# Fewer warm-up products, and a half slot's last tile in columns of 512 and 256 with its rows scattered in thirds

## The chip, the cores and the metric

One core of a Trainium2 chip runs the whole program. The metric is device time in microseconds (us). TensorE multiplies, ScalarE and VectorE empty its accumulators (PSUM) and prepare operands, GpSimd computes lists and issues the indirect DMAs (gathers and scatters of rows by an index), SyncE issues the plain loads.

## The reference, cut to what matters

Eight batches of 448 positions with 12 heads of 64 go through a sigmoid attention; its result, 3584 rows of 768, goes through a mixture of eight experts, of which each row takes one:

```python
scores = np.matmul(q, k.transpose(0, 1, 3, 2)) / 8 - np.log(448)
x = np.matmul(1 / (1 + np.exp(-scores)), v)   # then 3584 rows of 768
e_idx = np.argmax(x @ w_gate, axis=1)
for e in range(8):
    mask = e_idx == e
    h = np.maximum(x[mask] @ w1[e], 0.0)      # 768 -> 1024
    ye = h @ w2[e]                            # 1024 -> 768
    out[mask] = gate_w[mask, None] * eom[mask, e, None] * ye
```

## The kernel before

**Attention.** It comes first. `attention` runs over units of one 128-position chunk of keys for one pair of heads: `scores(u)` multiplies into one of two accumulators, ScalarE applies the sigmoid to it (L603), and two units later `values` multiplies by v. Ahead of the loop SyncE issues the first loads of q, k and v, and TensorE runs 20 products of a zeroed tile (L671 and L672), whose result nobody reads; the first `scores` stands behind them in TensorE's order and needs the first k and q.

**Slots.** The rows of one expert are taken in slots: big ones of 448 rows, then, for what is left of each expert, half slots of 256 rows (TM), under an `If` each. With these inputs two half slots run; the prediction calls them H0 and H1. `slot` writes out each engine's order by hand. In layer 1 (L537 on) eight column blocks of h are made; with the first four, GpSimd gathers the rows of the next slot, eight gathers of 32 x 4 row quarters for a half slot (`gather_rows`, L381), and w2 is split into a high and a low part. Behind layer 1 VectorE transposes the gathered rows (`turn_x`, L425), which needs all gathers landed, and they are split (`split_x`: a cast on ScalarE, L406, a subtraction on VectorE, L407). H1 does this too, for a slot that doesn't follow.

**Layer 2 of a half slot.** Two tiles of 128 rows, t = 0 and 1, each in two column halves, n = 0 and 1: four groups of 24 products of 384 columns, into one of three PSUM banks in turn. Behind a group ScalarE scales it by the row's weight into `y` (L490); in the last group of a half slot ScalarE scales 192 columns (L487) and VectorE the other 192 (L488). Between these scalings stand on ScalarE and VectorE the last `split_x` (behind the first group) and `split_w1` for the next slot (behind the first three). When both halves of a tile are in `y`, `scatter` (L495) issues one indirect DMA of its 128 rows of 3072 bytes into `out`. Scatters and gathers stand on GpSimd's one queue in the order of the code: the scatters of H0 ahead of the gathers of H1.

**Order between DMAs.** The framework puts in a semaphore wait where two instructions touch the same memory. `out` is written by every scatter; the indirect DMAs take eight completion semaphores (DMASW0 to DMASW7) in turn.

Of the kernel before, what the change touches and what calls it, by code (L numbers as in the profile page):

```python
# [11 lines left out]
I32 = mybir.dt.int32  # L12
AF = mybir.ActivationFunctionType
ALU = mybir.AluOpType
# [10 lines left out]
NT = B * S  # L25
# [6 lines left out]
TM = 256  # L32
# [19 lines left out]
def r32(ap):  # L52
    return ap.bitcast(F32)


class Kernel:
# [68 lines left out]
    def constants(self):  # L125
        nc = self.nc
        cp = self.const = self.pool("const")
        dram = self.pool("dram", space=DRAM)
        self.x_dram = dram.tile([NT, DM], F32, name="x_dram")
        self.lst = dram.tile([E * CAP, W], I32, name="lst")  # L130

        self.bias_s = cp.tile([128, 1], F32, name="bias_s")
        nc.vector.memset(self.bias_s, -math.log(S))
        nc.scalar.activation(self.warm_t(cp), self.bias_s, AF.Sigmoid)
        iota = lambda t, pattern, base=0, cm=0: nc.gpsimd.iota(
            t, pattern=pattern, base=base, channel_multiplier=cm, allow_small_or_imprecise_dtypes=True)
        self.rev = cp.tile([64, NB, E], F32, name="rev")
        iota(self.rev, [[0, NB], [-1, E]], E)
        self.last = cp.tile([64, 32], F32, name="last")
        nc.gpsimd.memset(self.last, 0.0)  # L140
        for i in range(2):
            iota(self.last[32 * i:32 * i + 32, 0:1], [[0, 1]], -1, CAP)
        self.step = cp.tile([64, 2], F32, name="step")
        self.turned = cp.tile([32, 32], F32, name="turned")
        self.run = cp.tile([1, E], F32, name="run")
        self.one = cp.tile([64, 1], F32, name="one")
        nc.gpsimd.memset(self.one, 1.0)
        self.ebase = cp.tile([1, E], F32, name="ebase")
        iota(self.ebase, [[CAP, E]])
        self.ids = cp.tile([1, E], F32, name="ids")  # L150
        iota(self.ids, [[1, E]])
        self.kts = cp.tile([1, KT], F32, name="kts")
        iota(self.kts, [[TB, KT]], TM)
        self.meta = cp.tile([128, B, NCH, W], I32, name="meta")
        for i in range(4):
            r, at = slice(32 * i, 32 * i + 32), HS * (i % 2) + 32 * NCH * (i // 2)
            for w, q, o in ((0, 4, 0), (1, 4, 1), (2, 4, 2), (3, 4, 3), (4, 1, 0)):
                nc.gpsimd.iota(self.meta[r, :, :, w], pattern=[[q * S, B], [q * 32, NCH]], base=q * at + o,
                               channel_multiplier=q)
        self.zero = cp.tile([128, 128], BF16, name="zero")  # L160
        nc.gpsimd.memset(self.zero, 0.0)
        self.eps = cp.tile([64, NB], F32, name="eps")
        nc.gpsimd.memset(self.eps, 1e-9)
        self.one8 = cp.tile([1, E], F32, name="one8")
        nc.gpsimd.memset(self.one8, 1.0)
        self.taken = cp.tile([1, E], F32, name="taken")
        nc.gpsimd.memset(self.taken, 0.0)
        self.tab_e, self.scattered = [], []
        slots = EARLY + LATE_N
        self.lts = cp.tile([128, slots, 4, 2], I32, name="lts")  # L170
        self.ltb = cp.tile([128, E, 2, 2], I32, name="ltb")
        self.lxs = cp.tile([128, slots, GB_], I32, name="lxs")
        self.lxb = cp.tile([128, E, GM], I32, name="lxb")
        self.slots = cp.tile([1, 2, LATE_N], F32, name="slots")
        for i, st in enumerate((1, TB)):
            iota(self.slots[:, i], [[st, LATE_N]])
        self.route_tiles()
# [296 lines left out]
    def layer2(self, s, t, n, y, last=False):  # L474
        nc = self.nc
        tk = slice(128 * t, 128 * t + 128)
        c = slice(384 * n, 384 * n + 384)
        hh, hl = self.hs
        ps = self.take("y", self.psy)[:, 0:384]
        for f in range(8):  # L480
            wh, wl = self.w2_at(f, c)
            nc.tensor.matmul(ps, hh[:, f, tk], wh, start=(f == 0), stop=False)  # L482
            nc.tensor.matmul(ps, hh[:, f, tk], wl, start=False, stop=False)  # L483
            nc.tensor.matmul(ps, hl[:, f, tk], wh, start=False, stop=(f == 7))  # L484
        w = r32(s["lt"][:, t, 1:2])
        if last and n == 1:
            nc.scalar.activation(y[:, 384:576], ps[:, 0:192], AF.Copy, scale=w)  # L487
            nc.vector.tensor_scalar(y[:, 576:768], ps[:, 192:384], w, None, ALU.mult)  # L488
        else:
            nc.scalar.activation(y[:, c], ps, AF.Copy, scale=w)  # L490
        if n == 1:
            self.scatter(s["lt"][:, t, 0:1], y)

    def scatter(self, at, y):
        self.nc.gpsimd.indirect_dma_start(  # L495
            out=self.out, out_offset=bass.IndirectOffsetOnAxis(ap=at, axis=0),
            in_=y, in_offset=None, bounds_check=NT - 1, oob_is_err=False)

    def layer2_rest(self, s):
        nc = self.nc  # L500
# [14 lines left out]
    def slot(self, cur, nxt, side=None, begun=False, hint=None):  # L515
        nx = None
        if nxt is not None:
            nx, rows, sure = nxt() if callable(nxt) else nxt
            last = -(-nx["lx"].shape[1] // 2) - 1
        n = 32 * cur["lx"].shape[1]  # L520
        for f in range(8):
            if n == TB and f == begun:
                self.change_step()
            self.layer1(f, n, begun and f == 0)
            if nx is not None and f <= last:
                self.gather_rows(nx, 2 * f, rows, 1)
                self.gather_rows(nx, 2 * f + 1, rows, 0)
                if f == last and not sure:
                    self.nc.gpsimd.drain()
            if side is not None:  # L530
                next(side, None)
            if 1 <= f < 5:
                self.split_w2(f - 1)
                if f > 1:
                    self.load_w1(nx, f - 2)
        for k in range(3):
            self.turn_x(nx, k)  # L537
        self.split_x(nx, 0)
        self.split_x(nx, 1)
        for i in range(2 * (n // 128)):  # L540
            t = i // 2
            if hint is not None and i == 5:
                more = self.nc.values_load(self.more[0:1, hint[1]:hint[1] + 1], engines=[ET.PE], min_val=0, max_val=1)
                self.tc.mark_branch_hint_location(hint[0], hint=more, engines=[ET.PE])
            self.layer2(cur, t, i % 2, self.ys[(t + (t > 0 and n % 128 > 0)) % 2], n == TM and t == 1)
            if i == 0:
                self.split_x(nx, 2)
            if i < 3 and nx is not None:
                self.split_w1(i)
                for k in range(i, 4 if i == 2 else i + 1):  # L550
                    self.load_w2(nx, k)
            if side is not None:
                next(side, None)
            if i == 1 and n % 128:
                self.layer2_rest(cur)
        return nx

    def attention(self, pool):
        nc = self.nc
# [4 lines left out]
        t = lambda n, shape: pool.tile(shape, F32, name=n)  # L564
# [3 lines left out]
        at = [t(f"a{i}", [128, 2, S]) for i in range(3)]  # L568
# [19 lines left out]
        def load_v(g):  # L588
            b, hp = divmod(G * g, NPAIR)
            v = vv[g % 3]  # L590
            nc.sync.dma_start(v[:, :, 0:3], self.vm[b, hp:hp + G].rearrange("g p c j d -> p g c j d"))
            for i in range(G):
                nc.sync.dma_start(v[half[i], i, 3], self.ve[b, hp + i])
# [74 lines left out]
        for g in (1, 2):  # L668
            load_qk(g)
            load_v(g)  # L670
        for _ in range(20):  # L671
            nc.tensor.matmul(self.ps_o[1][0][:, 0:256], warm[:, 0:128], warm, start=True, stop=True)  # L672
        LAG = 2
        for u in range(U * NG + LAG):
            g, i = divmod(u, U)
# [169 lines left out]
```

## Time and profile before

| | us |
|---|---|
| median of 3 runs | 773.86 |
| lowest, highest | 773.79, 775.93 |
| the profiled execution | 774.47 |
| its span, first to last instruction | 772.7 |
| TensorE busy | 759.8 |
| ScalarE, VectorE, GpSimd busy | 374.2, 398.9, 263.4 |

Times in rows are from the start of the span. A busy TensorE is not TensorE at its peak. A timeline row has start, duration, engine, line, operation, output and inputs, and in brackets how long the engine had been idle and what ended that. "POOLq" and "PEldq" are the queues that feed GpSimd and TensorE's weight loads: an event there is a wait for semaphores, which may stand beside work that was issued ahead of it. "DMA to landing" is the time from the start of the issuing instruction to the last semaphore increment.

### The profile page before, as it was taken

The numbers are of one execution on the slowest core, as the hardware profiler recorded it, in microseconds if no ns is written. First come the engines' busy times: TensorE is split into PE (matmuls) and PEld (weight loads), VectorE is DVE, ScalarE is ACT, GpSimd is POOL, SyncE is SP. The second block draws the span as 40 slices with busy tenths as digits, with TensorE's granted clock in tenths as the row PEclk, the third lists the DMA queues.
The fourth block names the chain that finished last, engine by engine and source line by source line (L and its number), as shares of the span: only waits on it lengthen the run. The fifth ranks groups of instructions, "written<-read, shape, count | busy, mean of one in ns | idle before, by whom it ended". The sixth has DMA issues, their size and how long they took to land. (4 is left out here: it accounts for less than half of the span.)

```text
span 772.7 us, 14875 instructions
## 1 busy us (share of the span) xinstructions
PE 759.8 (98%) x5826; PEld 585.0 (76%) x5826; DVE 398.9 (52%) x715; ACT 374.2 (48%) x429; POOL 263.4 (34%) x375
## 2 busy tenths in 40 slices
PE   9999999999999999999999999999999999989996
PEld 4444444444434389999999999999999999989996
DVE  1364646556686769523624615615615615614564
ACT  5666666666777733422523523524424524424454
POOL 5002112020443346258346137127127127215161
PEclk9999999999999999999999999999999999999998
DMA  8474756656796546447346346346345354354531
GB/s 283 122 212 130 208 138 176 188 149 171 261 300 200 143 108 200 137 110 222 114 154 215 113 137 215 118 135 210 115 139 176 116 174 155 103 195 151 181 137 41
DMA packets 73464, 126.53 MB, mean 164 GB/s; under 512 B 15375, under 2 KB 53263, under 8 KB 73376
## 3 DMA queue, kind: packets, MB, share of 16 engines
q1 hardware_dynamic: 62768, 100.18, 42.8%
q0 software_dynamic: 9680, 24.53, 9.5%
q8 instruction: 50, 0.82, 0.4%
q10 hardware_dynamic: 928, 0.69, 0.4%
q14 instruction: 38, 0.31, 0.1%
HBM read 108.77 MB, written 23.09 MB: 171 GB/s over the span
## 5 line engine op out<-in xcount | busy, mean ns | idle before, releaser
L603 ACT ACTIVATE a<-ps,bias_s 128x896 f32<-128x896 f32 x168 | 168.8, 1007 | 86.6 <-PE ps L601 86.0
L381 POOL DMA_INDIRECT plain<-x_dram,lxs x112 | 137.1, 1224 | 74.5 <-ACT h L467 24.3
L601 PE MATMUL ps<-q,k 64*64 64x448 f32 x1344 | 157.7, 540 | 0.7 <-ACT a L603 0.7
L610 PE MATMUL ps<-a,v 64*64 64x448 f32 x1344 | 156.2, 536 | 0.0
L455 PE MATMUL ps<-rounded 128*128 128x448 f32 (+1 forms) x432 | 151.3, 350 | 2.8 <-ACTq L798 2.8
L457 PE MATMUL ps<-rounded 128*128 128x448 f32 (+1 forms) x432 | 150.6, 349 | 0.0
L456 PE MATMUL ps<-rounded 128*128 128x448 f32 (+1 forms) x432 | 150.5, 348 | 0.0
L482 PE MATMUL ps<-w2h,h 128*128 128x384 f32 x400 | 133.9, 335 | 0.3 <-DVE y L512 0.2
L484 PE MATMUL ps<-w2h,h 128*128 128x384 f32 x400 | 133.7, 334 | 0.0
L483 PE MATMUL ps<-w2l,h 128*128 128x384 f32 x400 | 133.6, 334 | 0.0
L468 DVE SCALAR_TENSOR_TENSOR h<-ps,h 128x384 fp32r<-128x384 f32 (+2 forms) x128 | 45.2, 390 | 164.0 <-ACT h L467 164.0
L407 DVE TENSOR_TENSOR rounded<-plain,rounded 128x2048 fp32r<-128x2048 f32 (+5 forms) x63 | 97.6, 1570 | 55.2 <-ACT rounded L406 55.0
L467 ACT ACTIVATE h<-ps 128x448 fp32r<-128x448 f32 (+1 forms) x72 | 36.7, 510 | 162.0 <-PE ps L457 158.9
L601 PEld LDWEIGHTS ps<-q,k 64*64 64x64 f32 x1344 | 50.6, 134 | 76.0 <-issue 70.3
L610 PEld LDWEIGHTS ps<-a,v 64*64 64x64 f32 x1344 | 51.4, 133 | 74.9 <-issue 72.4
L406 ACT CAST rounded<-plain 128x2048 fp32r<-128x2048 f32 (+5 forms) x63 | 83.0, 1333 | 28.3 <-DVE plain L425 26.4
L495 POOL DMA_INDIRECT out<-y,lts x28 | 31.7, 1133 | 186.0 <-ACT y L490 125.3
L455 PEld LDWEIGHTS ps<-rounded 128*128 128x128 f32 x432 | 82.3, 191 | 8.6 <-ACTq L798 3.1
L457 PEld LDWEIGHTS ps<-rounded 128*128 128x128 f32 x432 | 82.2, 190 | 5.0
L456 PEld LDWEIGHTS ps<-rounded 128*128 128x128 f32 x432 | 82.2, 190 | 4.9
L482 PEld LDWEIGHTS ps<-w2h,h 128*128 128x128 f32 x400 | 75.1, 188 | 1.1 <-DVE y L512 0.5
L483 PEld LDWEIGHTS ps<-w2l,h 128*128 128x128 f32 x400 | 75.1, 188 | 0.1
(141 smaller groups left out, 680.9 us busy)
## 6 DMA issues: line engine op xcount, KB each, us to landing
plain<-w SPq DMA_DIRECT2D x40, 768.0 KB, 4.8
plain<-w SPq DMA_DIRECT2D x27, 1024.0 KB, 5.1
k<-kT SPq DMA_DIRECT2D x23, 448.0 KB, 3.5
q<-qT SPq DMA_DIRECT2D x23, 448.0 KB, 6.2
x_dram<-xt SPq DMA_DIRECT2D x30, 336.0 KB, 5.8
v<-vm SPq DMA_DIRECT2D x24, 384.0 KB, 5.3
plain<-w SPq DMA_DIRECT2D x6, 512.0 KB
plain<-x_dram,lxs POOLq DMA_INDIRECT x112, 4.4
```

What stands on the lines that cost most here:

```text
L381: self.paced(self.nc.gpsimd.indirect_dma_start(out=self.xg[:, g], out_offset=None, in_=x4, in_offset=bass.IndirectOffsetOnAxis(ap=s["lx"][ ...
L406: self.nc.scalar.copy(hi, raw)
L407: self.nc.vector.tensor_tensor(lo, raw, r32(hi), ALU.subtract)
L455: nc.tensor.matmul(ps, wh[d][:, c], xh[:, d, 0:n], start=(d == 0), stop=False)
L456: nc.tensor.matmul(ps, wh[d][:, c], xl[:, d, 0:n], start=False, stop=False)
L457: mm = nc.tensor.matmul(ps, wl[d][:, c], xh[:, d, 0:n], start=False, stop=(d == 5))
L482: nc.tensor.matmul(ps, hh[:, f, tk], wh, start=(f == 0), stop=False)
L483: nc.tensor.matmul(ps, hh[:, f, tk], wl, start=False, stop=False)
L484: nc.tensor.matmul(ps, hl[:, f, tk], wh, start=False, stop=(f == 7))
L601: qk = nc.tensor.matmul(ps[half[h], j, 0:S], k[half[j], e, o:o + 64], q[half[j], e], start=True, stop=True)
L603: self.beat[0] = nc.scalar.activation(at[u % 3], ps[:, :, 0:S], AF.Sigmoid, bias=self.bias_s, scale=1.0 / math.sqrt(D)).ins
L610: nc.tensor.matmul(self.ps_o[e][h][half[j], 0:S], v[half[h], e, c, j], a[half[h], j], start=(i in ((0, 3 if h else 4)[e],)), stop=(i == (2 ...
```

## The change

**Start.** The loop of warm-up products runs 11 times instead of 20.

**Half slots' last tile.** `layer2` with `last` (only t = 1 of a half slot) takes columns 0 to 512 and 512 to 768 instead of two halves of 384. ScalarE scales both alone; VectorE's part (L488) goes. The tile's rows are scattered in thirds of 256 columns (1024 bytes a row): two scatters behind the first group, one behind the second. The output is seen as 10752 rows of 256 for that, and the row numbers 3 * row + k are made by three 128x1 operations on VectorE (`third_rows`), behind `split_x(nx, 2)`. Tile 0 and the big slots scatter whole rows as before.

```diff
+        self.thirds = cp.tile([128, 3], I32, name="thirds")
...
     def layer2(self, s, t, n, y, last=False):
...
-        c = slice(384 * n, 384 * n + 384)
+        c = slice(*((0, 512), (512, 768))[n] if last else (384 * n, 384 * n + 384))
...
-        ps = self.take("y", self.psy)[:, 0:384]
+        ps = self.take("y", self.psy)[:, 0:c.stop - c.start]
...
-        w = r32(s["lt"][:, t, 1:2])
-        if last and n == 1:
-            nc.scalar.activation(y[:, 384:576], ps[:, 0:192], AF.Copy, scale=w)
-            nc.vector.tensor_scalar(y[:, 576:768], ps[:, 192:384], w, None, ALU.mult)
-        else:
-            nc.scalar.activation(y[:, c], ps, AF.Copy, scale=w)
-        if n == 1:
+        nc.scalar.activation(y[:, c], ps, AF.Copy, scale=r32(s["lt"][:, t, 1:2]))
+        if last:
+            for k in range(c.start // 256, c.stop // 256):
+                self.scatter(self.thirds[:, k:k + 1], y[:, 256 * k:256 * k + 256], 3)
+        elif n == 1:
             self.scatter(s["lt"][:, t, 0:1], y)
 
-    def scatter(self, at, y):
+    def third_rows(self, at):
+        for k in range(3):
+            self.nc.vector.tensor_scalar(self.thirds[:, k:k + 1], at, 3.0, float(k), ALU.mult, ALU.add)
+
+    def scatter(self, at, y, parts=1):
         self.nc.gpsimd.indirect_dma_start(
-            out=self.out, out_offset=bass.IndirectOffsetOnAxis(ap=at, axis=0),
-            in_=y, in_offset=None, bounds_check=NT - 1, oob_is_err=False)
+            out=self.out.rearrange("n (i e) -> (n i) e", i=parts),
+            out_offset=bass.IndirectOffsetOnAxis(ap=at, axis=0),
+            in_=y, in_offset=None, bounds_check=parts * NT - 1, oob_is_err=False)
...
             if i == 0:
                 self.split_x(nx, 2)
+                if n == TM:
+                    self.third_rows(cur["lt"][:, 1, 0:1])
...
-        for _ in range(20):
+        for _ in range(11):
```

GpSimd's queue at the end of H0 and the start of H1's gathers, with the semaphores that each instruction waits for (`y_..` is a tile's scaled rows, `ltb` holds row numbers, `lxb` the next slot's gather indices). Before:

```order
L381 DMA plain<-x_dram,lxb 128x192 [waits DMASW3_49,Activation_49]
L495 DMA out<-y_2665,ltb 3584x768 [waits DMASW4_49,Activation_49,Pool_49]
L495 DMA out<-y_2666,ltb 3584x768 [waits DMASW5_49,DMASW4_49,DVE_49]
L805 COMPARE_AND_BRANCH
L381 DMA plain<-x_dram,lxb 128x192 [waits DMASW6_49,PE_49]
L381 DMA plain<-x_dram,lxb 128x192 [waits DMASW7_49,Activation_49]
```

GpSimd's queue at the same place after the change:

```order
L382 DMA plain<-x_dram,lxb 128x192 [waits DMASW3_49,Activation_49]
L498 DMA out<-y_2657,ltb 3584x768 [waits DMASW4_49,Activation_49,Pool_49]
L498 DMA out<-y_2658,thirds 10752x256 [waits DMASW4_49,DMASW5_49,DVE_49,Activation_49]
L498 DMA out<-y_2658,thirds 10752x256 [waits DMASW6_49,DMASW5_49,DVE_49]
L498 DMA out<-y_2658,thirds 10752x256 [waits DMASW6_49,DMASW7_49,DVE_49,Activation_49]
L811 COMPARE_AND_BRANCH
L382 DMA plain<-x_dram,lxb 128x192 [waits DMASW0_49,PE_49]
```

Tile 0's scatter completes on DMASW4 and the ones behind it on DMASW5, 6 and 7; each waits for the earlier use of its own semaphore, and for that of the scatter ahead of it. Three scatters stand where one stood, ahead of H1's gathers.

VectorE in layer 2 of H0, behind the transposes of the gathered rows. Before:

```order
L407 TENSOR_TENSOR rounded<-plain,rounded 128x2x256 [waits PE_49,Activation_49] x3
L407 TENSOR_TENSOR rounded<-plain,rounded 128x2048 [waits DMAHW5_49,Activation_49]
L407 TENSOR_TENSOR rounded<-plain,rounded 128x2048 [waits DMAHW6_49,Activation_49]
L407 TENSOR_TENSOR rounded<-plain,rounded 128x2048 [waits DMAHW7_49,PE_49,Activation_49]
L488 TENSOR_SCALAR y_2666<-ps,ltb 128x192 [waits Activation_49,Pool_49]
```

VectorE at the same place after the change:

```order
L408 TENSOR_TENSOR rounded<-plain,rounded 128x2x256 [waits PE_49,Activation_49] x3
L495 TENSOR_SCALAR thirds<-ltb 128x1 [waits Pool_49]
L495 TENSOR_SCALAR thirds<-ltb 128x1 x2
L408 TENSOR_TENSOR rounded<-plain,rounded 128x2048 [waits DMAHW5_49,Activation_49]
L408 TENSOR_TENSOR rounded<-plain,rounded 128x2048 [waits DMAHW6_49,Activation_49]
L408 TENSOR_TENSOR rounded<-plain,rounded 128x2048 [waits DMAHW7_49,PE_49,Activation_49]
```

The three index operations stand ahead of the splits of w1, and the scaling behind them is gone. ScalarE's order is as before, with 512 and 256 columns in the last two scalings.

## Rows read from the trace of the kernel before

**Rows 1.** The page, busy us, share of the span, instructions.
```profile
PE 759.8 (98%) x5826; PEld 585.0 (76%) x5826; DVE 398.9 (52%) x715; ACT 374.2 (48%) x429; POOL 263.4 (34%) x375
```
**Rows 2.** ScalarE's timeline, second scaling of H0, then three of H1.
```profile
723.70 0.58 ACT L490 ACTIVATE y<-ps,ltb 128x384 f32<-128x384 f32 x1
...
757.62 0.58 ACT L490 ACTIVATE y<-ps,ltb 128x384 f32<-128x384 f32 x1 [1.27 <-PE ps L484]
...
765.94 0.42 ACT L487 ACTIVATE y<-ps,ltb 128x192 f32<-128x192 f32 x1 [1.79 <-PE ps L484]
```
**Rows 3.** VectorE's timeline, transposes of H0 and H1, last scaling of H1.
```profile
718.86 1.90 DVE L425 STREAM_TRANSPOSE plain<-plain 128x512 f32<-128x512 f32 x3 [2.64 <-DMA plain<-x_dram,lxb]
...
750.50 1.90 DVE L425 STREAM_TRANSPOSE plain<-plain 128x512 f32<-128x512 f32 x3 [0.37 <-DMA plain<-x_dram,lxb]
...
766.40 0.42 DVE L488 TENSOR_SCALAR y<-ps,ltb 128x192 f32<-128x192 f32 x1
```
**Rows 4.** GpSimd's timeline, scatters of H0 and H1, first and last gather of H1.
```profile
725.11 1.78 POOL L495 DMA_INDIRECT out<-y,ltb  x1 [11.85 <-ACT y L490]
...
734.55 0.98 POOL L381 DMA_INDIRECT plain<-x_dram,lxb  x1 [0.30 <-issue]
...
747.48 0.94 POOL L381 DMA_INDIRECT plain<-x_dram,lxb  x1 [0.31 <-issue]
758.48 1.09 POOL L495 DMA_INDIRECT out<-y,ltb  x1 [10.06 <-ACT y L490]
767.10 0.99 POOL L495 DMA_INDIRECT out<-y,ltb  x1 [7.53 <-DVE y L488]
```
**Rows 5.** Views of L495 at 767, 758, 725, 679; of L381 at 700, 741.
```profile
DMA to landing us min/median/max: 3.7/3.7/3.7
...
L495 POOLq EVENT_SEMAPHORE  x1: 4671/4671/4671, 758.3 to 758.3; - x1
...
DMA to landing us min/median/max: 4.5/4.5/4.5
...
DMA to landing us min/median/max: 6.6/6.6/6.6
...
DMA to landing us min/median/max: 3.0/3.0/3.0
...
DMA to landing us min/median/max: 2.6/2.7/2.7
...
L381 POOL DMA_INDIRECT plain<-x_dram,lxb x4: 942/1851/1860, 741.0 to 747.5; - x4
...
DMA to landing us min/median/max: 3.6/3.8/3.8
```
**Rows 6.** A big slot: view of L495 at 672, timelines of VectorE and GpSimd.
```profile
L495 POOLq EVENT_SEMAPHORE  x1: 6633/6633/6633, 672.1 to 672.1; - x1
...
677.56 0.61 DVE L512 SCALAR_TENSOR_TENSOR y<-ps,lts,y 64x384 f32<-64x384 f32 x1 [0.93 <-ACT y L511]
...
679.51 0.93 POOL L495 DMA_INDIRECT out<-y,lts  x1 [5.71 <-issue]
```
**Rows 7.** Start: views of L672, L601; TensorE's timeline; then 697 to 700.3 (windows, L455).
```profile
L672 PE MATMUL ps<-rounded x20: 415/415/582, 1.2 to 5.5; 128*128 128x256 f32 x20
...
L601 PEldq EVENT_SEMAPHORE  x1: 51/51/51, 4.5 to 4.5; - x1
...
L601 PE MATMUL ps<-q,k x16: 537/774/1006, 5.8 to 7.8; 64*64 64x448 f32 x16
...
6.60 1.35 PE L601 MATMUL ps<-q,k 64*64 64x448 f32 x8
...
8.70 0.61 PE L601 MATMUL ps<-q,k 64*64 64x448 f32 x4 [0.37 <-ACT a L603]
...
697.00:700.30 3.30, 3.30 (x17) 3.30 (x17) 0.00 (x0) 0.30 (x1) 0.00 (x0) 0.50 0.18 70
...
L455 PE MATMUL ps<-rounded x5: 415/415/419, 697.1 to 699.7; 128*128 128x256 f32 x5
```

## The prediction, made before the change was run

> **What bounds the kernel now.** I read the page's busy times first: TensorE is busy for 98% of the span [rows 1], so until the last product the time is TensorE's, and whatever moves its first real product moves the end by as much. Then the timelines of the last stretch, ScalarE's, VectorE's and GpSimd's: the kernel ends on a scatter of result rows, not on a product. Two half slots run; call them H0 and H1. In H1 ScalarE scales the first half of the last columns at 765.94 for 0.42, VectorE's part starts only at 766.40 for 0.42 [rows 2, 3], the scatter starts at 767.10 [rows 4] and lands 3.7 later, at 770.8 [rows 5]; the span ends at 772.7, so 1.9 lie behind the last landing.
>
> Next I read what a scatter waits for, in the view of its line. GpSimd's queue stands from 758.3 for 4.67 us, that is until 762.97, at a wait that belongs to the last scatter; the scatter of the tile before it started at 758.48 and lands 4.5 later, at 762.98 [rows 4, 5]. In a big slot it costs time today: the wait from 672.1 lasts 6.63, to 678.7, VectorE had finished those rows at 678.17, and the scatter starts at 679.51 [rows 6]. So a scatter into `out` waits until the scatter before it has landed, and starts 0.8 later. Before the change that hides behind products. In the program after it, the order in front.md shows each third waiting for the semaphore of the third before: three scatters that follow each other by landing plus 0.8.
>
> **The change part by part.**
>
> *Eviction and products of the last tile.* 24 products of 512 and 24 of 256 columns replace 48 of 384: as many products and as many columns, so TensorE's end stays, and 512 or 256 columns are costed at zero by both counts. ScalarE's two scalings end 8.32 apart over two groups of products [rows 2], 4.16 each, so the wider group ends a third later: its scaling starts near 757.62 + 5.55 = 763.2 and, from 0.42 for 192 and 0.58 for 384 columns [rows 2], takes 0.69; the last takes 0.47 instead of 0.42 + 0.42 on two engines. By itself that gives back 0.4. The three 128x1 index operations lie on VectorE between splits where it waits for ScalarE; zero.
>
> *One landing of a third (131 KB).* Not in the trace. Nearest rows: a 98 KB gather lands in 2.7, a 64-row scatter of 196 KB in 3.0, both on quiet queues [rows 5]; I take 2.8. Beside weight loads a whole tile takes 6.6, and gathers beside VectorE's splits 3.8 [rows 5]: the upper ends. The Trainium skill, DMA: Bandwidth & Descriptors, Anatomy of one DMA, gives a fixed 2.0 us plus bytes over 436 KB per us. By that slope the 196 KB scatter's 3.0 would become 2.85 for a third, and a third would land 0.6 before a whole tile; by it the sum below would be 0.1 higher, and the three thirds still pay the fixed part three times.
>
> *H0: the thirds delay H1's gathers.* The first tile's scatter of H0 starts at 725.11 and lands 6.6 later, at 731.7 [rows 4, 5]; third A starts at 732.5 (its columns are scaled by 730). Weight loads still fill the DMA engines; between 2.8 and 6.6 I take 5.0: A lands at 737.5, B starts at 738.3 and takes 3.8, C starts at 742.9. The eight gathers of H1 stand behind C on GpSimd's queue. C lies beside VectorE's splits and takes 1.85, as the gathers there do [rows 5]; with the 0.3 between two of GpSimd's DMAs [rows 4] the first gather starts at 745.05 and not at 734.55, 10.5 late. Before, the eight take 13.9 because most lie beside those splits; now one does (2.15 with its gap), the others take 1.25, so the eighth starts at 754.7, lands at 757.4, and VectorE's transposes begin at 757.7 instead of 750.50 [rows 3, 4]: 7.2 late.
>
> *H1: ScalarE's queue.* Behind the transposes stand, on ScalarE in order, two casts of x, the first scaling, two casts, the second scaling. In H0 that took 4.84 from transposes to second scaling (718.86 to 723.70) [rows 2, 3] with nothing idle between. So H1's second scaling starts at 757.7 + 4.84 = 762.55, not 757.62. TensorE doesn't feel it: its last group needs the bank of the first scaling, free by 760.7, and starts after 763. But the first tile's scatter starts 1.4 (H0) or 0.9 (H1) after that scaling began [rows 2, 4]; with 1.2 at 763.75. It lands in 3.0 to 4.5 [rows 5]; 3.7 gives 767.45.
>
> *H1: the chain of thirds.* A at 767.45 + 0.8 = 768.25 (its columns are scaled by 765.7); B at 768.25 + 2.8 + 0.8 = 771.85; C at 775.45, landed at 778.25; with the 1.9 behind it the span ends at 780.2. The tail costs 7.5.
>
> Its ends: A in H0 at 2.8 instead of 5.0, B and C there at 3.0, the first tile at 3.0 and 0.9 put the end near 777.2 (+4.5); A in H0 at 6.6, the first tile at 4.5 and H1's thirds at 3.8 each put it at 784.7 (+12.0).
>
> *Eleven warm-up products.* Twenty start between 1.2 and 5.5 at 0.22 each; 256 columns take 415 ns there, and the first score products 1006 falling to 537 ns by 7.8 [rows 7]: the pace of 1.2 GHz, then of 2.4 (at 697 to 700, where the profile has a granted clock of 0.50, 256 columns also take 415 [rows 7]; the page's clock row shows full speed from the start, so here I go by the products). The nine that go took 9 x 0.213 = 1.9. The last semaphore that the first score product needs is passed at 4.5 [rows 7], so it can start at about 4.5 instead of 5.80, and TensorE stands from 3.8 to 4.5. At the low level a unit of scores takes two rounds of 0.75 to 0.8 (5.80 to 6.60 is the first [rows 7]), two units 3.05: 7.56. The third starts at 8.70 now, when ScalarE has finished the first unit [rows 7]; then it could start at 7.56, 1.1 earlier. That is the gain if the clock rises when it does now, near 7.4. If instead it rises as long after the first product without a gap as now (6.2 after 1.23, so at 10.7), then from 7.56 to 10.7 every us does half its work: 1.57 lost, 0.4 slower in all. I take +0.4, since the pause is new and nothing before it had raised the clock by 4.5; bounds -1.1 and +0.6. The Trainium skill, TensorE: Matmul & The Clock Gate, What's actually happening, says that activity releases the clock and that the monitor doesn't start anew with the kernel, so the point differs between executions. By that the term would vary between my two values from run to run; one trace can't show it.
>
> *Sum.* 7.5 + 0.4 = 7.9. The profiled execution took 774.47 for a span of 772.7, so 1.8 lie around the span; it would take 782.4. It is 0.6 above the median, 773.86, which becomes 781.8.
>
> **The rivals.** (1) *Only H1's thirds count.* If H1's gathers start so little late that the transposes begin before 752.8 (2.3 late), ScalarE catches up. Then the first tile's scatter lands at 762.98 as now, A starts at 763.2 + 0.69 + 0.28 = 764.15, B at 767.75, C at 771.35, landed at 774.15, end 776.1: +3.4, and with the start 777.7. Against it: H0's first tile lands only at 731.7, so C can't be out before 739 even at 2.8 each. (2) *The thirds flow as meant*, the other side: A and B lie under the last 2.9 us of products and C starts 0.28 after the last scaling, at 766.7, carries a third and lands in 2.8: end 771.4, -1.3; with +0.4 it gives 773.0, with -1.1 it gives 771.5, faster. It decides only if two links fit between 764.15 and 766.7, under 1.3 each, or if the wait isn't for the landing; the shortest link in the rows is 2.7 + 0.8. (3) *Worse:* thirds slow in H1 too, 786. (4) *The clock rises as early as now:* the forecast less 1.5, 780.3; it changes no sign but in rival 1, where it gives 776.2.
>
> **How the numbers follow.** The forecast, 781.8 (777 to 785): 0.72, of which a third has the early clock. Rival 1: 0.15. Rival 2: 0.06. Rival 3: 0.07. The range 777.0 to 785.0 leaves out rivals 2 and 3 and the lower third of rival 1, 0.18. About 0.3%, 2.3 us, is what a measurement of this kernel can tell from no change: faster below 771.5, slower above 776.2. Rival 2 with the early clock gives faster 0.03; its rest and rival 1 with the early clock give same 0.08; slower 0.89.
>
> **What would show it.** On GpSimd: in each half slot four scatters that start one landing plus 0.8 apart, 3.6 in H1; H1's first gather at about 745; the transposes at about 758; ScalarE's second scaling near 762.5. TensorE's last product near 766 as now, and some 14 us between it and the end instead of 7. At the start the first score product at 4.5 and the third unit at 7.6, and a pace of 1006 ns that lasts past 7.5. The forecast is wrong if a third starts before the one ahead of it has landed, or if the last product moves by more than 2.

## The result and the profile after the change

The changed kernel takes 782.29 us (781.52 to 783.84), the kernel before 774.55 (773.79 to 775.93) beside it: a ratio of 1.0114 [1.0099, 1.0128]. The medians lie 7.7 apart; the ratio would be 8.8 us, and the two profiled spans lie 9.2 apart. The forecast was 781.8 in 777 to 785. The total came out by luck: the change of the half slots was taken some 2 us too cheap or more, the shorter start 1 to 2 us too dear.

The profiled execution of after took 783.84 with a span of 781.9. The page's busy times, to be held against [rows 1]:

```profile
PE 759.3 (97%) x5817; PEld 582.1 (74%) x5817; DVE 398.5 (51%) x719; ACT 374.0 (48%) x429; POOL 272.2 (35%) x379
```

GpSimd's timeline (start us, us, what; in brackets the idle time before and what ended it), to be held against [rows 4]:

```profile
725.00 1.77 POOL L498 DMA_INDIRECT out<-y,ltb  x1 [11.84 <-ACT y L486]
732.47 2.28 POOL L498 DMA_INDIRECT out<-y,thirds  x1 [5.70 <-ACT y L486]
739.48 1.83 POOL L498 DMA_INDIRECT out<-y,thirds  x1 [4.73 <-issue]
743.51 2.13 POOL L498 DMA_INDIRECT out<-y,thirds  x1 [2.20 <-ACT w2h L407]
745.94 1.86 POOL L382 DMA_INDIRECT plain<-x_dram,lxb  x1 [0.30 <-issue]
...
764.01 2.46 POOL L498 DMA_INDIRECT out<-y,ltb  x1 [7.43 <-ACT y L486]
769.76 1.33 POOL L498 DMA_INDIRECT out<-y,thirds  x1 [3.29 <-DMA out<-y,ltb]
774.20 0.97 POOL L498 DMA_INDIRECT out<-y,thirds  x1 [3.10 <-issue]
777.36 0.97 POOL L498 DMA_INDIRECT out<-y,thirds  x1 [2.20 <-DMA out<-y,thirds]
```

In both half slots four scatters now stand 3.2 to 7.5 us apart, and GpSimd is idle between them. The first gather of H1 starts at 745.94 and not at 734.55. GpSimd's busy time rose by 9 us, which costs nothing by itself; the spacing is the cost. In the chain of what ended last stands a third's landing, 2.31 after its start:

```profile
774.20 2.31 DMA out<-y,thirds
```

The views of the other scatters of H1 have 2.5 for the last third, 3.7 for the first and 4.8 for the tile ahead of them (764.01):

```profile
DMA to landing us min/median/max: 2.5/2.5/2.5
...
DMA to landing us min/median/max: 3.7/3.7/3.7
...
DMA to landing us min/median/max: 4.8/4.8/4.8
```

VectorE's timeline, the transposes of H1, which start 7.9 later than in [rows 3]:

```profile
758.44 1.90 DVE L426 STREAM_TRANSPOSE plain<-plain 128x512 f32<-128x512 f32 x3 [7.72 <-DMA plain<-x_dram,lxb]
```

ScalarE's timeline, the second and the last scaling of H1, to be held against [rows 2]:

```profile
763.16 0.57 ACT L486 ACTIVATE y<-ps,ltb 128x384 f32<-128x384 f32 x1
...
767.79 0.48 ACT L486 ACTIVATE y<-ps,ltb 128x256 f32<-128x256 f32 x1
```

TensorE hardly feels it. By its timeline the last product starts at 766.18; then 15.7 us pass to the end at 781.9:

```profile
766.18 0.28 PE L485 MATMUL ps<-w2h,h 128*128 128x256 f32 x1
```

TensorE's timeline at the start of after, the counterpart of [rows 7]:

```profile
1.23 2.71 PE L678 MATMUL ps<-rounded 128*128 128x256 f32 x11 [1.23 <-DVE rounded L671]
4.14 3.87 PE L607 MATMUL ps<-q,k 64*64 64x448 f32 x24 [0.19 <-DMA q<-qT]
8.04 0.98 PE L616 MATMUL ps<-a,v 64*64 64x448 f32 x8
```

The value products (L616) start at 8.04; in the kernel before they start at 9.50, behind the third unit of scores at 8.70 [rows 7]. The start was a gain and not the small loss that I had chosen. TensorE's waits in after (line waited for: total, times, longest) show, beside 0.2 for the first q, two that the kernel before does not have:

```profile
PE ps L513 <- ACT y L486: 1.3, 1, 1.3
...
PE ps L458 <- DVE rounded L408: 0.4, 1, 0.4
```

The first lies at 371 us, in a big slot that the diff does not touch, the second in layer 1 of H1. The experiments take them up.

### The profile page after: what moved, and what is told of

It is laid out like the page before. It is cut to its first block, busy times and chain, and to the rows that moved or that the text cites. A ratio compares the mean times of both kernels' runs of the same rounds, so it can differ in the third digit from the quotient of the medians.

```text
span 781.9 us, 14874 instructions
## 1 busy us (share of the span) xinstructions
PE 759.3 (97%) x5817; PEld 582.1 (74%) x5817; DVE 398.5 (51%) x719; ACT 374.0 (48%) x429; POOL 272.2 (35%) x379
## 5 line engine op out<-in xcount | busy, mean ns | idle before, releaser
L382 POOL DMA_INDIRECT plain<-x_dram,lxs x112 | 140.1, 1251 | 73.5 <-ACT h L468 23.0
L616 PE MATMUL ps<-a,v 64*64 64x448 f32 x1344 | 156.4, 537 | 0.0
L483 PE MATMUL ps<-w2h,h 128*128 128x384 f32 (+2 forms) x400 | 134.1, 335 | 0.3 <-DVE y L516 0.2
L485 PE MATMUL ps<-w2h,h 128*128 128x384 f32 (+2 forms) x400 | 134.0, 335 | 0.0
L484 PE MATMUL ps<-w2l,h 128*128 128x384 f32 (+2 forms) x400 | 133.9, 335 | 0.0
L616 PEld LDWEIGHTS ps<-a,v 64*64 64x64 f32 x1344 | 51.4, 133 | 75.1 <-issue 72.3
```

The costliest lines, as they stand in the source:

```text
L382: self.paced(self.nc.gpsimd.indirect_dma_start(out=self.xg[:, g], out_offset=None, in_=x4, in_offset=bass.IndirectOffsetOnAxis(ap=s["lx"][ ...
L616: nc.tensor.matmul(self.ps_o[e][h][half[j], 0:S], v[half[h], e, c, j], a[half[h], j], start=(i in ((0, 3 if h else 4)[e],)), stop=(i == (2 ...
```

## The experiments

Kernels that ran on one chip share the runs of the kernel before there. Its median differs from chip to chip (774.14, 773.63, 776.57, 776.82), so each result names the one beside it, and medians are compared within one chip unless the text says otherwise.

**Eleven warm-up products alone.** The kernel before with

```diff
-        for _ in range(20):
+        for _ in range(11):
```

> The kernel before with 11 warm-up products and nothing else changed. In the two traces the unit of scores that waited for ScalarE came at 7.04 instead of 8.70, and ScalarE stayed about 1.4 us ahead until 316 us; at 371 us it was 0.26 ahead, and TensorE, which ran on, stood 1.3 us there. Theory: the first big slot's transposes wait for gathers whose indices come through a row of list loads and copies that doesn't start earlier, so nearly all of the gain is given back there: 0.0 to 0.3 us faster than before at the end. Rival, the step as predicted (what moves TensorE's first product moves the end by as much): with the early rise of the clock 1.1 to 1.5 us faster.

Measured: 772.65 against 774.14, ratio 0.998 [0.9968, 0.9992]; span 770.7. The 1.5 us reach the end; the expectation that they are swallowed at 371 us fell. ScalarE's rows in this trace lie 2.1 to 2.8 ahead of the kernel before from 220 us to the last slot, and TensorE has no wait at 371. So the 1.3 there in after was not the start's doing in general; the same wait (1.4) stands in one later trace without thirds. It comes and goes between executions, and I did not find what decides it.

**Everything else.** The changed kernel with `range(20)`.

> The kernel after with 20 warm-up products: the tail's change alone. Theory (start given back at 371 us, tail costs all): within 0.3 us of the kernel after, 7.5 to 8.2 us slower than before. Rival (the start is worth 1.1 to 1.5 at the end): 1.1 to 1.5 slower than the kernel after, about 9 slower than before.

Measured: 785.38, ratio to before 1.0132 [1.0103, 1.0161]; span 783.4, 1.5 above after's. The rival came true: the start is worth something at the end. The edits of the half slots by themselves lose 11.2 us in the medians (four executions, 782.42 to 785.73) and 10.2 by the ratio.

**Thirds that don't wait for each other.** The changed kernel, with the scatters of one slot declared independent (they write different places; this frees the scatters of the big slots too):

```diff
+        for j in self.outs:
+            self.tc.declare_no_dep(i, j, reason="tiles and thirds of one slot go to different places")
+        self.outs.append(i)
```

> The kernel after, with the scatters of one half slot declared to go to different places, so that none waits for the one before it; the same products, scalings and scatters in the same order. Theory (the waits for landings are the whole cost): the thirds start one GpSimd instruction apart, H1's gathers start near 736, its transposes near 751, the last third starts 0.3 after the last scaling and lands in about 2.5; the end comes 0.5 to 1.5 us before that of the kernel before, 8 to 9 before that of the kernel after. Rival (three scatters cost by their number, on GpSimd or the DMA engines): at least 3 us slower than the kernel before, with H1's gathers still late.

Measured: 775.17, ratio 1.0019 [1.0007, 1.0031]; span 773.5. GpSimd's timeline, H1's first gather and the thirds of H1:

```profile
733.74 0.98 POOL L382 DMA_INDIRECT plain<-x_dram,lxb  x1 [0.30 <-PE ps L458]
...
763.36 0.99 POOL L498 DMA_INDIRECT out<-y,thirds  x1 [4.50 <-ACT y L486]
764.66 0.97 POOL L498 DMA_INDIRECT out<-y,thirds  x1 [0.30 <-issue]
766.01 2.03 POOL L498 DMA_INDIRECT out<-y,thirds  x1 [0.38 <-ACT y L486]
```

The wait for the landing was nearly the whole loss: without it the thirds leave 1.3 apart, H1's gathers are early again, and 7.1 of after's 782.29 are gone (medians from two chips). But the gain over before that I had expected here is missing: against the kernel with 11 products alone, 2.5 us are left (775.17 to 772.65). No wait between thirds is left in this kernel to explain them; the experiment on the columns shows most of them.

**Thirds in the second half slot only.** H0 as before.

> The kernel after, but the first half slot's last tile in two halves of 384 columns with one scatter as before; 512 and 256 columns and thirds from the second half slot on. Theory (two costs: H0's thirds hold back H1's gathers and with them ScalarE's queue, H1's own chain of thirds comes on top): transposes of H1 near 750 as before, and of the 7.7 us that the kernel after is slower 2.5 to 3.5 stay. Rival (H1's chain alone is the cost): all 7.7 stay.

Measured: 777.26, ratio 1.0038 [1.0025, 1.0051]; span 773.9. Against the kernel with 11 products alone it is 3.2 by the spans and 4.6 by the medians; the profiled execution is the fastest of its nine. Here A starts at 761.64, B at 765.00, C at 769.65: two links lie under the last products and only the last one sticks out. It is rival 1 of the prediction, which had 3.4 for it.

**Thirds in the first half slot only.** The reverse.

> The changed kernel with thirds in the first half slot alone; the second has columns, scaling and one scatter as before. Theory: the late gathers of the second half slot reach the end even without thirds there, by way of ScalarE's queue and the first tile's scatter, which starts near 763 and lands near 767.5; the last scatter waits for that until 768.3 instead of starting at 765.0 as in the kernel with 11 warm-up products alone, and lands in 2.7 to 3.75. So 2.4 to 3.4 slower than that kernel's 772.65: 775.0 to 776.0. Rival: late gathers are hidden as long as TensorE is not late, only the 0.7 of the late w1 part stays: 773.0 to 773.7.

Measured: 777.30 against 773.63, ratio 1.0053 [1.0035, 1.0071]; span 775.2; the theory had 775.0 to 776.0. GpSimd, H1's first gather and the two scatters of H1:

```profile
744.87 1.85 POOL L382 DMA_INDIRECT plain<-x_dram,lxb  x1 [0.31 <-issue]
...
762.97 2.46 POOL L504 DMA_INDIRECT out<-y,ltb  x1 [7.45 <-ACT y L492]
770.01 0.99 POOL L504 DMA_INDIRECT out<-y,ltb  x1 [4.58 <-DVEq L817]
```

The late gathers reach the end without any third in H1, although TensorE waits for none of them. ScalarE's scalings of H1 come late, and the first tile's scatter starts at 762.97; its landing, at 769.2, lets the last scatter go at 770.01. (The row names VectorE's queue. VectorE's own part of the last scaling, late behind its splits, ends at 769.41, so without the landing the scatter would start only some 0.3 earlier.) There is a second way, which I had overlooked: SyncE's last weight loads go into a buffer that VectorE's last split sets free, and the late transposes make this split late. At its end SyncE waits only 0.5 for the last scatter (the row names GpSimd's queue by a gather):

```profile
SPq L853 <- DMA plain<-x_dram,lxb: 0.5, 1, 0.5
```

So most of what H0's thirds cost would stay even if the last scatter were earlier.

The single traces also differ ahead of the half slots. That drops out when one counts from ScalarE's last scaling in H0 to the end of the span. This scaling before:

```profile
732.02 0.42 ACT L487 ACTIVATE y<-ps,ltb 128x192 f32<-128x192 f32 x1 [1.79 <-PE ps L484]
```

And in after:

```profile
731.90 0.47 ACT L486 ACTIVATE y<-ps,ltb 128x256 f32<-128x256 f32 x1 [0.35 <-PE ps L485]
```

From there it is 40.7 before and 40.8 and 40.9 in the two traces of 11 products alone; 50.0 in after and 51.4 with 20 products; 44.4 with thirds in H0 alone, 44.3 in H1 alone, and 42.9 with independent thirds. Thirds, with the columns that go with them, thus cost 3.6 in H0, 3.5 in H1, and 9 to 11 together: the late first tile takes away the cover under which two of the three links lie when H1's thirds stand alone. By medians, which come from several chips, the excess over the sum is not clear of noise.

**The columns alone.** The kernel before with

```diff
-        c = slice(384 * n, 384 * n + 384)
+        c = slice(*((0, 512), (512, 768))[n] if last else (384 * n, 384 * n + 384))
...
-        if last and n == 1:
-            nc.scalar.activation(y[:, 384:576], ps[:, 0:192], AF.Copy, scale=w)
-            nc.vector.tensor_scalar(y[:, 576:768], ps[:, 192:384], w, None, ALU.mult)
```

> The kernel before with the 512 and 256 columns scaled by ScalarE alone; 20 warm-up products, one scatter for the whole last tile. Theory, from the run without the waits between scatters, which stayed 2.5 us behind the kernel that only shortens the warm-up: the wide scaling pushes ScalarE's cast of the last part of w1 behind it, so TensorE enters the second half slot's layer 1 about 0.7 late; the last scaling gives back 0.4; and the same late cast puts a VectorE split (2.3 us) beside the last scatter, whose GpSimd instruction then takes 2.0 instead of 1.0. Together 1.3 slower than before: 775.0 to 775.9, with a landing 4.5 or more after the last scatter's start. Rival, the prediction's step: columns cost nothing and the eviction gives 0.4, 773.5 to 774.0.

Measured: 775.45 against 773.63, ratio 1.003 [1.0017, 1.0042]: 1.8 slower, within the theory's 775.0 to 775.9, where the prediction had 0.4 faster. ScalarE's timeline in H0:

```profile
727.98 0.69 ACT L486 ACTIVATE y<-ps,ltb 128x512 f32<-128x512 f32 x1 [2.27 <-issue]
728.57 1.89 ACT L406 CAST rounded<-plain 128x2048 fp32r<-128x2048 f32 x1
```

One of TensorE's waits, which the kernel before does not have:

```profile
PE ps L457 <- DVE rounded L407: 0.4, 1, 0.4
```

VectorE's timeline at the end of H1:

```profile
765.41 2.29 DVE L407 TENSOR_TENSOR rounded<-plain,rounded 128x2048 fp32r<-128x2048 f32 x1 [3.58 <-PE ps L484]
```

GpSimd's timeline there, and behind it a line from the view of that scatter:

```profile
766.23 2.34 POOL L491 DMA_INDIRECT out<-y,ltb  x1 [7.17 <-ACT y L486]
...
DMA to landing us min/median/max: 5.3/5.3/5.3
```

Behind the wide scaling on ScalarE stands the cast of the last part of w1. The wide scaling starts a third of a group of products later, so the cast does, and VectorE's split of what it rounds, and TensorE waits for that split in layer 1 of H1. From ScalarE's rows TensorE loses 0.7 there in this trace and in the one without waits between thirds. In H1 the same late split runs from 765.41 to 767.70 and so beside the last scatter, whose GpSimd instruction takes 2.34 instead of 0.99 [rows 4], and which lands 5.3 after its start instead of 3.7 [rows 5]. The Trainium skill, SBUF — State Buffer, Who interferes with whom, says that a VectorE instruction with two inputs in SBUF contends with a GpSimd instruction that reads SBUF; the split is such an instruction, and the trace agrees.

The end of this trace is not the scatter's, though: no wait for a DMA stands at SyncE's end. The late split holds back SyncE's last loads, which are issued by 768.23 and not by 767.00:

```profile
767.73 0.50 SPq L392 DMA_DIRECT2D plain<-w  x2
```

From there to the end it is 5.5. Counted from ScalarE's last scaling in H0 the end comes 42.9 later, as with independent thirds, and 2.2 more than before. So the thirds themselves, once independent, cost nothing that these traces show; the columns do.

**Two warm-up products.** The kernel before with `range(2)`.

> The kernel before with 2 warm-up products instead of 20. Theory, from four traces with 11 in which the granted clock rises at 6.1 to 7.7 us although TensorE stood still before the first score product: the rise does not depend on what these products do, so 2 are as good as 11: the first score product at 4.0 to 4.2 as there, the rise at 6 to 8 us, and 772.3 to 773.2. Rival: the products do raise the clock, and with 2 of them (0.5 us of work, then 2.3 us of standing) it rises as long after the first score product as it did after the first warm-up product in the kernel before, 6.2, so near 10.3; half of the work between 7.0 and 10.3 is then lost, 1.6, and it takes 774.0 or more.

Measured: 773.23 against 773.63, ratio 1.0001 [0.9986, 1.0017]: a time between the two forecasts, with the late rise of the rival. TensorE's timeline:

```profile
1.24 0.79 PE L672 MATMUL ps<-rounded 128*128 128x256 f32 x2 [1.24 <-DVE rounded L665]
4.03 4.76 PE L601 MATMUL ps<-q,k 64*64 64x448 f32 x24 [2.00 <-DMA q<-qT]
8.53 1.65 PE L610 MATMUL ps<-a,v 64*64 64x448 f32 x8
10.00 0.94 PE L601 MATMUL ps<-q,k 64*64 64x448 f32 x8
```

TensorE's timeline in the kernel with 11 products alone:

```profile
1.24 2.72 PE L672 MATMUL ps<-rounded 128*128 128x256 f32 x11 [1.24 <-DVE rounded L665]
4.03 2.74 PE L601 MATMUL ps<-q,k 64*64 64x448 f32 x16
6.92 0.98 PE L601 MATMUL ps<-q,k 64*64 64x448 f32 x8 [0.15 <-ACT a L603]
```

Eight products take 1.65 at the pace of 1.2 GHz and 0.94 at that of 2.4. After two warm-up products and 2.0 us of standing the slow pace lasts to 10.00; after eleven it ends before 6.92. (Each timeline's 0.94 or 0.98 is eight products.) In every trace with eleven the pace had turned by 8.0; with two there is one trace. In these traces the warm-up does help to raise the clock, and eleven products are enough for it.

**Halves, independent.** From what went before I built a version: 11 products, columns and scaling as before, the last tile's rows scattered in halves of 384 columns, each as soon as it is scaled, and scatters of a slot independent.

> A version built on what the first four runs show: 11 warm-up products; columns and scaling of the last tile as before (384 and 384, the second split over ScalarE and VectorE); the last tile's rows scattered in halves, each as soon as its 384 columns are scaled, and scatters of one half slot declared independent, so none waits for another's landing. Theory: TensorE's work and the order on ScalarE are those of the kernel with 11 warm-up products alone (772.65), the last scatter starts as there, 0.3 after the last scaling, and carries 196 KB, which the 64-row scatter of the same size landed in 3.0, instead of 3.75 for 393 KB: 771.4 to 772.1. Rival: the shorter transfer does not shorten the end, or the additional scatter on GpSimd's queue delays it: 772.5 to 773.5.

Measured: 773.42 against 773.63, ratio 0.9998 [0.9987, 1.0009]; span 772.4. The gain that I expected is not there. Repeated on another chip, beside 11 products alone and halves with 20 products:

> The kernel before with 11 warm-up products once more, beside the two that follow on one chip, so that warm-up and tail can be read as two edits with four corners (the kernel before is the fourth). Theory: 1.0 to 1.8 faster than before, as in its first run (1.5), whatever the tail is. Rival: the first run's 1.5 was mostly the chance of where the granted clock rose and fell, and here it is 0 to 0.7.

> The version with halves and 11 warm-up products once more. Its first trace has the last scatter landing 3.04 after its start instead of 3.6 to 3.8, but reaches the last scaling 1.85 after the kernel with 11 warm-up products alone, of which 1.2 arose where the clock stood at half for 6.8 us near 694 instead of 3.4. Theory: that was chance and the halves are worth 0.5 to 0.8: 0.5 to 0.8 below the kernel with 11 products alone on this chip. Rival: the halves' further scatter costs what it gains, and the two agree within 0.3, or this one is slower.

> Halves and independent scatters with 20 warm-up products as before. Theory: 0.5 to 0.8 below the kernel before, and 1.0 to 1.8 above the same with 11. Rival: no difference from before within 0.3, if the shorter last transfer does not shorten the end.

Measured, against 776.57: 775.88 for 11 products alone (0.9992 [0.9975, 1.001]), 777.55 for halves with 11 (1.0009 [0.9992, 1.0025], without one of its twelve executions, which took 1102.43), 778.30 for halves with 20 (1.002 [1.0002, 1.0038]). Nine products fewer give 0.7 in either pair, the upper end of the rival's 0 to 0.7 and not the 1.0 to 1.8 of the theory. Halves lose 1.7 in either pair, where I had expected a gain of 0.5 to 0.8. The last one changed nothing but the start and the second half slot:

> 11 warm-up products, and halves of the last tile with independent scatters only in the second half slot; big slots and the first half slot as before, so that nothing but the start differs until the last 20 us. The version with halves everywhere lost its gain ahead of the half slots, between 270 and 720 us. Theory: that loss comes with the big slots' independent scatters or is chance, and the end's gain (landing in 3.0 instead of 3.6 to 3.8) shows here: 0.5 to 0.8 below what 11 warm-up products alone give (0.7 to 1.5 below before in two runs), together 1.2 to 2.3 below before. Rival: the shorter landing does not shorten the end, and it stays 0.7 to 1.5 below before, or less.

Measured: 776.42 against 776.82, ratio 0.9993 [0.9981, 1.0005]: the rival.

Why the halves bring nothing shows at the end. GpSimd's timeline in the halves' first trace, and the line of GpSimd's closing waits, the last of which passes at 769.9 when that scatter has landed, 3.1 after its start:

```profile
766.79 0.97 POOL L502 DMA_INDIRECT out<-y,thirds  x1 [3.46 <-DVE y L489]
...
L819 POOLq EVENT_SEMAPHORE  x4: 17/43/43, 767.0 to 769.9; - x4
```

The closing waits of the kernel before end at 770.8, 3.7 after its last scatter started [rows 4]:

```profile
L805 POOLq EVENT_SEMAPHORE  x4: 17/43/43, 767.3 to 770.8; - x4
```

The scatter starts 0.3 earlier than before and lands 0.9 earlier, yet the span ends only 0.3 earlier. SyncE's waits in the last stretch tell why (line waited for: total, times, longest). The kernel before:

```profile
SPq L805 <- SPq L805: 3.0, 1, 3.0
...
SPq L841 <- DMA plain<-x_dram,lxb: 0.2, 1, 0.2
```

The halves, where no wait for a DMA stands in the list:

```profile
SPq L819 <- SPq L819: 3.1, 1, 3.1
```

The changed kernel:

```profile
SPq L847 <- DMA plain<-x_dram,lxb: 5.8, 1, 5.8
```

SyncE issues the slot's last weight loads, then leaves the slot by a branch, stands 3 us, and works through its closing semaphores. In the kernel before it then waits 0.2 us for the last of GpSimd's DMAs (the row names the queue by a gather), in after 5.8, for the last third, and in the halves not at all: there SyncE's own chain is the later one. Its last loads are issued at 762.35 + 4.65 = 767.00 before and at 762.06 + 4.65 = 766.71 with halves. SyncE's timeline before:

```profile
762.35 4.65 SPq L392 DMA_DIRECT2D plain<-w  x3
```

And with halves:

```profile
762.06 4.65 SPq L393 DMA_DIRECT2D plain<-w  x3
```

From there to the end it is 5.7 in both. In the eight traces in which SyncE waits for no DMA at its end (11 products alone twice, independent thirds, the columns, halves three times, halves in H1) it lies between 5.5 and 5.9. A shorter last transfer alone could thus win 0.2 us.

What halves lose lies ahead of the last scatter. In the three later traces with halves (11 products, 20 products, halves in H1) the granted clock (1.00 is 2.4 GHz, 0.50 is 1.2) is 0.64, 0.63 and 0.68 between 280 and 284, after TensorE had stood for 1.8 of the 4 us before, while the kernel with 11 products alone, having stood as long, shows 1.00. Two stretches of halves in H1 (window, us, TensorE's busy time and products, granted clock, DMA share, GB/s):

```profile
276.00:280.00 4.00, 2.21 (x18) 0.89 0.90 205
280.00:284.00 4.00, 4.00 (x15) 0.68 0.39 118
```

The same stretches with 11 products alone, on another chip:

```profile
276.00:280.00 4.00, 2.21 (x27) 1.00 0.87 200
280.00:284.00 4.00, 4.00 (x22) 1.00 0.46 134
```

0.68 is a stretch partly at 1.2 GHz and partly at 2.4. By ScalarE's rows such a fall costs 1.6 us. Whether halves bring it about or it was chance in these traces stays open; the version with halves in H1 does the same work as 11 products alone up to its last slot, which speaks for chance. So does a second stretch: between 697 and 701 twelve of the fourteen traces, the kernel before among them, show 0.53 to 0.80, and this one of 11 products alone shows 1.00 again. In the second and third trace of halves TensorE also takes 1.2 longer through layer 1 of H1 than in the first, which I cannot explain.

Of all kernels tried, the one before with 11 warm-up products is the only one whose interval lies below 1 on a chip; its second run points the same way but does not confirm it (0.7 us, interval over 1). It is 0.7 to 1.5 us faster than the kernel before.

## Why the prediction was right, and where it was not

- *A scatter waits until the one ahead of it has landed.* Right; it carries the loss. In after a third starts 0.8 to 0.9 after the landing ahead of it (774.20 + 2.31 = 776.51, next start 777.36; forecast 0.8), and without the wait 7 us return. In H0 it costs by way of the late gathers.
- *H0's thirds delay H1's gathers.* Right. First gather 745.94 (forecast 745.05), transposes 758.44 (757.7), second scaling 763.16 (762.55), first tile's scatter 764.01 (763.75). The links in H0 were 7.0 and 4.0 from start to start; I had 5.8 and 4.6.
- *TensorE does not feel it.* Right for the gathers. H0's thirds alone make the kernel 3.7 us slower than before in the medians, and no wait of TensorE for a gather stands behind it. What I had not counted is that the late transposes also hold back VectorE's splits and with them SyncE's last loads.
- *The chain in H1.* The mechanism was right, the first link too short. The first tile's scatter was put at 3.7 and took 4.8; it now lies beside VectorE's splits (GpSimd 2.46 instead of 1.09 [rows 4]). With the same 2.46 it took 6.2 with thirds in H0 alone and 6.5 with 20 products, so the splits alone do not set it, and the 4.8 was on the lucky side. I had the row for that, 4.5 as an upper end, and did not ask what else moves beside a scatter that starts 5.5 us later. A third was put at 2.8; the three took 3.7, 2.3 and 2.5. The two on quiet queues are nearer to the figure of the Trainium skill, DMA: Bandwidth & Descriptors, Anatomy of one DMA: by 2.0 us plus bytes over 436 KB per us a third would take some 2.3, as an estimate, and the trace agrees. Forecast for the last landing 778.25, in the trace 777.36 + 2.5 = 779.9.
- *512 or 256 columns cost nothing, and the eviction gives back 0.4.* This step failed: it costs 1.8 (2.2 in the trace, from H0's last scaling on). I counted the columns on TensorE and the two scalings by themselves, and did not ask what is queued behind the wider scaling on ScalarE (the cast that VectorE's split and TensorE wait for), nor which loads wait for that later split.
- *Eleven warm-up products, +0.4.* This step failed: it gives 0.7 to 1.5. The first score product came at 4.14 (forecast 4.5; it waited for the first q only until then), and the 1.1 that I had for an early clock lies within what was measured; the choice of the late clock was wrong. I had reasoned that any pause starts the wait for the fast clock anew. The traces show that a stop as short as these 0.2 us does not; in the one with two products, with 2.0 us of standing and less work ahead of it, the clock did rise later. The Trainium skill, TensorE: Matmul & The Clock Gate, What's actually happening, says that activity releases the clock and that the point varies between executions. The trace agrees: with the same eleven products the first sixteen score products took 2.74 in one trace and 1.96 in the first one of halves. I had given the early clock a third of the forecast; the rows bear it out.
- *What lies behind the last landing, 1.9.* Right in after (781.9 - 779.9 = 2.0), where the last landing comes last. It holds only while SyncE's own chain ends first, which I had not looked at. Rival 2, the thirds as they were meant, had counted a landing 1.3 earlier as 1.3 of time; by SyncE's rows no more than 0.2 was to be had, so its price was wrong.
- *The sum.* 7.5 + 0.4 was forecast. By medians it is 7.7 over the kernel before: 8.4 to 9.2 for the tail, less 0.7 to 1.5 for the start; the run with 20 warm-up products has 11.2 for the tail alone, and the two traces with thirds in both half slots have 9.3 and 10.7 from H0's last scaling on. That the forecast hit was luck: the tail was taken too low and the start too high by about the same.

## What to carry to other kernels

Before a transfer is cut into pieces, look in the trace for a start that waits on the landing of the piece ahead: if there is one, each piece pays a whole landing and its start-up, and the cure is to declare the pieces independent, not to make them smaller. (Here that only took the loss away; it won nothing.) When an instruction on a queue gets longer, follow the next two or three behind it to the engines that wait for them; a scaling that looked 0.4 cheaper cost 1.8 through the cast behind it, the split behind that, and the loads that wait for the split. And before the last transfer is shortened, see whether another engine's closing chain ends at the same time.

## What the runs showed of the hardware

- The end of this kernel is held by two chains of nearly one length: the last landing plus 2.0, and SyncE's last loads plus 5.5 to 5.9. In the second, SyncE's first closing semaphore comes 3 us after the branch out of the slot (the 3.0 and 3.1 above; 2.6 to 3.3 over all traces). The Trainium skill, Runtime: NRT & Kernel Launch, Instruction fetch mechanics, says that a taken branch to a target which is not at hand stalls the engine for a fetch; the 3 us would fit, but no run here separates a fetch from other causes.
- The same GpSimd scatter took 0.99 in the kernel before and 2.34 in the one with the columns, and landed in 3.7 and 5.3. The difference that the timelines show is a VectorE split beside it in the second; the DMA engines were nearly idle in both (a share of 0.09 and 0.07 from 766 to 768).
- A stand of TensorE of the same length (1.8 us before 280) was followed by a granted clock of 0.63 to 0.68 in three traces and by 1.00 in another. Such a fall costs 1.6 us, as much as most edits of this study, so a difference of a microsecond between single traces says little here.
